# First attention layer of a four-layer attention and gMLP kernel: prologue order, weight burst, and two-tile residual loads

## The chip, the cores and the metric

The kernel runs on one core of a Trainium2 chip. The metric is the device time of one execution in microseconds (us). For each run except four early ones of the kernel before, the mean clock granted to TensorE is recorded as well, to three digits.

The engines are named as the profile names them: PE (TensorE matmuls), PEld (its weight loads), DVE (VectorE), ACT (ScalarE), POOL (GpSimd) and SP (SyncE). SPq, ACTq and POOLq stand for those engines' instruction queues when they issue a DMA.

## The reference

```python
x = A_x                                   # 2048 rows, 576 columns, bf16
x = x + A(layernorm(x))                   # attention, the layer that is changed
x = x + B(layernorm(x))                   # gMLP
x = x + A(layernorm(x))
x = x + B(layernorm(x))

def A(x):      # 32 heads of 18 columns; each row looks at 8 keys, 2 rows apart, behind it
    q, k, v = split(x @ wqkv)
    logits = sum(q[s] * k[s - 2*w] for the 18 columns) * 18**-0.5       # w = 0..7, masked at the start
    return (softmax(logits) @ v[s - 2*w]) @ wo

def B(x):      # F/2 = 2304
    z = gelu(x @ w_in)
    z1, z2 = z[:, :2304], layernorm(z[:, 2304:])
    return (z1 * (w_sp @ z2 + b_sp[:, None])) @ w_out
```

## The kernel before: what the change touches

The attention layer works in 19 row blocks t of 112 new rows, each in two steps (16 heads each), so steps s = 0 to 37. A step computes logits (`L_mm`, PE), exponentials (`EXP`, ACT) and the weighted values (`PV`, PE). A table hangs other PE work into the steps: query and key projections (`PG`), value projections (`VW`), output projections (`WO`).

Queries and keys need another layout than the projection leaves: each head at a multiple of 32 partitions. So `PG` evacuates into a staging tile, and DMAs of up to 18 partitions and 72 KB ("QK moves" below; half the size in the fifth block of columns) carry it into `QK`. Two of the staging tiles are lent by the later gMLP weight tile `win2a`; moves out of those are called QK<-win2a in the profile, moves from the others QK<-stg.

```python
# PG, when a staging tile is full: columns d*128.., half cb of the rows
for dst, src in moves:                                   # 18 partitions, 2 x 1024 columns of bf16
    dma_rr[0] += 1
    self.dma(dst, src, eng=queues[dma_rr[0] % len(queues)])     # POOL and SP in turn
...
def fill_window_rows(self, QK, half):                    # DVE copies of the window mask's rows into QK
...
# prologue of the first layer (cut): S_ statistics, E_/R_ 1/std, A_ normalize, T_pe transpose on PE
T_pe(0)                    # 5 transposes on PE, then an ACT copy into xnT
VW(0, 0, False)
VW(0, 1, False)
S_(2)
A_(1)
T_pe(1)
VW(1, 0, False)
S_(3)
...
rows[2](nc.scalar)         # ACT issues the store of the mask's rows, win_period
A_(2, 3)
T_pe(2)
T_pe(3)
VW(1, 1, False)
...
self.load_pat(nc.sync)     # reads win_period back
...
order = [(d, 0) for d in range(4)] + [(d, 1) for d in range(4)] + [(4, 0), (4, 1)]
for k_, (d, cc) in enumerate(order):                     # projections of the first 1024 rows
    for qk in ((1, 0) if d < 4 else (0,)):
        PG(d, qk, cc, False, (nc.gpsimd, nc.sync) if d in (0, 4) else q2)
...
T_(12, 13, 14, 15)         # DMA transposes, issued by SP
nvw0, nvw = 4, 8
...
self.fill_window_rows(QK, 1)                             # window rows of the second half

# the table: which PE work goes into which step
PG_END = 14
pre, pgs = pgs[:6], pgs[6:]
for k_, (d, qk, cc) in enumerate(pgs):                   # 12 projections of the last 1024 rows
    at((k_ * PG_END) // len(pgs), PG, d, qk, cc, True)
for t in range(nvw, NT):
    for hh in range(2):
        at(2 * t - 2 + hh, VW, t, hh, 2 * t - 2 + hh >= PG_END and hh == 0)
for i in range(NS):                                      # 16 tiles of 128 rows
    t = -(-(i + 1) * P // QT) - 1
    s = 2 * t + (6 if li == 0 and t < 8 else 5 if t < NT - 5 else 4 if t < NT - 3 else 3)
    at(s - 5, XO, i)       # SP loads the residual rows, one tile
    at(s, WO, i, 0)        # waits for oT<-o_t, a DMA transpose that SP issues
    at(s + 1, WO, i, 1)
    ...
    at(s + 4, LN_T, i)     # DMA transpose of the next layer's input, issued by SP
at(0, self.load_wo, nc.sync)
for k_, f in enumerate(self.load_win2a(nc.gpsimd)):      # six loads of 288 KB, issued by POOL
    at(5 + 2 * k_, f)
...
L_mm(0)
EXP(0)
for d, qk, cc in pre:      # six projections ahead of the logits of step 1
    PG(d, qk, cc, li > 0, q2)
for s in range(NST):
    if s + 1 < NST:
        L_mm(s + 1)
        EXP(s + 1)
    PV(s)
    for f, a in table.pop(s, []):
        f(*a)
```

The softmax here doesn't subtract the row's maximum and nothing guards it: scores larger than these inputs give would overflow.

## Time and profile before

| | before |
|---|---|
| median of the first three runs | 1196.32 us (1195.26 to 1196.66) |
| span of the profiled run | 1193.5 us, granted clock 0.999 |
| PE busy | 1180.0 us, 99% |
| PE idle outside the first 130 us | about 1 us (the second attention layer) and the tail |

From the page of the kernel before: the head and the first row of part 1 (busy time, share of the span, instructions), the clock row of part 2 (tenths of full speed in 40 slices), and part 4 (the chain that ended last, by engine).

```profile
span 1193.5 us, 20790 instructions
PE 1180.0 (99%) x8554; PEld 620.5 (52%) x8554; DVE 545.4 (46%) x1202; ACT 378.5 (32%) x597; POOL 274.3 (23%) x382
PEclk9999999999999999999999999999999999999999
PE 94%; DMA 1%; ACT 0%; issue 0%; DVE 0%; DVEq 0%; ACTq 0%
```

PE is the bound, so only time in which PE waits, or runs at a lower clock, can be won. The list of PE's waits (what waited, for whom: us in total, times, longest) is short:

```profile
PE pv L377 <- ACT xnT L567: 3.0, 3, 1.4
PE L_ps L435 <- ACT P_sb L444: 2.3, 6, 0.4
PE L_ps L435 <- DMA QK<-win2a: 1.9, 3, 1.0
...
PE pw L489 <- DMA oT<-o_t: 1.0, 1, 1.0
PE pw L489 <- DVE rec L461: 0.3, 1, 0.3
```

All but the exponentials' waits of the second attention layer lie in the first 110 us. The costliest place is at 47 us. The PE timeline there (start, duration, instruction, in brackets the idle time before it and what ended it):

```profile
47.86 0.20 PE L435 MATMUL L_ps<-QK 32*128 32x112 bf16 x1 [0.23 <-DMA QK<-win2a]
48.71 0.40 PE L435 MATMUL L_ps<-QK 32*128 32x112 bf16 x8 [0.65 <-DMA QK<-win2a]
50.08 0.22 PE L435 MATMUL L_ps<-QK 32*128 32x112 bf16 x1 [0.97 <-DMA QK<-win2a]
...
50.66 2.29 PE L400 MATMUL pp<-xnT,wqk_sb 128*128 128x512 bf16 x5
```

The logits of step 1 wait three times for the last QK moves. The projection that follows takes 2.29 us where the next takes 1.27: the records of the clock show one stretch of 3.41 us at half clock, 50.54 to 53.95 us. Such stretches are called half-clock windows below. One of them lowers the mean clock by 0.5 * 3.41 / 1193.5 = 0.0014.

What POOL and DVE did just before (their timelines; x5 means five instructions in a row, the duration covers all five):

```profile
41.77 4.82 POOL L77 DMA_DIRECT2D QK<-win2a  x5 [1.29 <-DMA QK<-stg]
40.88 4.62 DVE L197 COPY QK<-win_pat 128x4096 bf16<-128x4096 bf16 x4
```

POOL's five last move issues took 4.82 us, 0.96 us each in the mean, while DVE copied the window rows. Two more lines of this kernel are needed for the comparison below: the wait of an output projection at 104 us, and SP's issue of the last four QK moves.

```profile
104.10 0.79 PE L489 MATMUL pw<-wo_sb,oT 128*128 128x288 bf16 x5 [0.97 <-DMA oT<-o_t]
81.60 3.18 SPq L77 DMA_DIRECT2D QK<-stg  x4
```

### The profile page before, as it was taken

To read this page: it belongs to the slowest core of one execution; us is meant where nothing else is said; L and a number is where in the kernel's file an instruction comes from. 1 tells how busy PE (TensorE), PEld (TensorE's weight loads), DVE (VectorE), ACT (ScalarE), POOL (GpSimd) and SP (SyncE) were. 2 spreads that over 40 slices of the span, in tenths; PEclk is the share of its full clock that TensorE was granted. 3 is DMA by queue.
4 is the path that set the end of the run, shared out by engine and by line. 5 is a ranking of instruction groups with operands and counts; after the bars stand their busy time and mean duration, and the time that the engine had idled before them with its cause. 6 is when DMAs were issued, how large, how long until landed. Compare 5 with 4: busy or idle time off the path is not lost.

```text
span 1193.5 us, 20790 instructions
## 1 busy us (share of the span) xinstructions
PE 1180.0 (99%) x8554; PEld 620.5 (52%) x8554; DVE 545.4 (46%) x1202; ACT 378.5 (32%) x597; POOL 274.3 (23%) x382
## 2 busy tenths in 40 slices
PE   8999999999999999999999999999999999999998
PEld 5566644444444444457755775444444444444676
DVE  8577677333233233244455786763233233233321
ACT  5578677211111111201156786770110110111000
POOL 3568773100000000001153877530000000000000
PEclk9999999999999999999999999999999999999999
DMA  8799792000000000049645799900000000001332
GB/s 195 140 191 238 172 228 58 23 1 12 12 12 12 12 1 12 2 140 294 169 99 113 189 239 197 209 12 11 12 12 1 12 12 12 12 1 31 121 105 73
DMA packets 178791, 101.21 MB, mean 85 GB/s; under 512 B 135039, under 2 KB 160047, under 8 KB 178696
## 3 DMA queue, kind: packets, MB, share of 16 engines
q1 hardware_dynamic: 165400, 78.14, 29.4%
q0 software_dynamic: 6480, 15.99, 5.3%
q10 hardware_dynamic: 6816, 5.77, 1.6%
q8 instruction: 67, 1.10, 0.4%
q14 instruction: 28, 0.23, 0.1%
HBM read 42.39 MB, written 16.53 MB: 49 GB/s over the span
## 4 chain that ended last, share of the span: by engine, by line
PE 94%; DMA 1%; ACT 0%; issue 0%; DVE 0%; DVEq 0%; ACTq 0%
PE pg L878 42%; PE pz L860 12%; PE po L932 12%; PE pz L782 11%; PE pp L400 4%; PE pw L489 3%; PE O_ps L455 3%; PE pv L377 3%; PE L_ps L435 2%; PE pzs L782 1%; ACT P_sb L444 0%; DMA QK<-win2a 0%; DMA oT<-o_t 0%; PE pt L473 0%; DVE ln_st L218 0%
## 5 line engine op out<-in xcount | busy, mean ns | idle before, releaser
L878 PE MATMUL pg<-Wq,Z 128*128 128x512 bf16 x2304 | 502.8, 379 | 0.0
L878 PEld LDWEIGHTS <-Z 128*128 128x128 bf16 x2304 | 225.1, 98 | 272.2
L882 DVE TENSOR_TENSOR g_tmp<-pg,ln_xn 128x512 f32<-128x512 f32 x144 | 99.6, 692 | 428.0 <-PE pg L878 428.0
L872 ACT ACTIVATE z1T<-pz 128x1024 bf16<-128x1024 f32 x72 | 73.7, 1023 | 513.9 <-PE pz L860 513.7
L77 POOL DMA_DIRECT2D wout<-in_B_w_out_dram x4 | 4.2, 1060 | 604.6 <-PE pg L878 604.6
L932 PE MATMUL po<-wout,Z 128*128 128x288 bf16 x1152 | 141.4, 286 | 0.0
L444 ACT ACTIVATE P_sb<-L_ps 128x896 bf16<-128x896 f32 (+1 forms) x152 | 126.7, 888 | 41.8 <-PE L_ps L435 41.1
L860 PE MATMUL pz<-xnT,w 128*128 128x512 bf16 (+1 forms) x640 | 136.0, 380 | 0.0
L932 PEld LDWEIGHTS <-Z 128*128 128x128 bf16 x1152 | 112.7, 98 | 28.8
L782 PEld LDWEIGHTS <-xnT 128*128 128x128 bf16 (+1 forms) x800 | 66.3, 97 | 80.9 <-issue 23.7
L782 PE MATMUL pz<-win2a,xnT 128*128 128x512 bf16 x384 | 104.8, 380 | 0.0
L883 DVE TENSOR_TENSOR Z<-g_tmp,z1T 128x512 bf16<-128x512 f32 x144 | 99.7, 692 | 10.8 <-DVE g_tmp L882 1.4
L860 PEld LDWEIGHTS <-w 128*128 128x128 bf16 (+1 forms) x640 | 51.1, 97 | 80.0 <-issue 27.1
L400 PE MATMUL pp<-xnT,wqk_sb 128*128 128x512 bf16 x360 | 83.5, 382 | 0.0
L796 ACT ACTIVATE zp<-pz 128x1024 bf16<-128x1024 f32 x64 | 65.5, 1023 | 36.7 <-PE pz L782 34.1
L242 POOL TENSOR_SCALAR ln_xn<-x_new,ln_mv,ln_rstd 128x576 bf16<-128x576 f32 x32 | 73.3, 2291 | 2.7
L942 DVE TENSOR_TENSOR x_new<-po,xo 128x288 f32<-128x288 f32 (+1 forms) x64 | 28.8, 456 | 87.9 <-PE po L932 83.7
L782 PE MATMUL pz<-win2b,xnT 128*128 128x512 bf16 (+1 forms) x256 | 65.8, 380 | 0.0
L798 DVE CUSTOM_DVE_ANT_0 Z<-zp 128x1536 bf16<-128x1536 bf16 x32 | 56.3, 1760 | 16.2 <-ACT zp L796 16.1
L77 POOL DMA_DIRECT2D QK<-stg x81 | 50.0, 620 | 40.7 <-ACT P_sb L444 14.3
L377 PE MATMUL pv<-wv_sb,xnT 128*128 128x288 bf16 (+1 forms) x380 | 56.2, 285 | 3.0 <-ACT xnT L567 3.0
L400 PEld LDWEIGHTS <-wqk_sb 128*128 128x128 bf16 x360 | 33.3, 98 | 36.6 <-issue 0.8
(111 smaller groups left out, 889.0 us busy)
## 6 DMA issues: line engine op xcount, KB each, us to landing
xres<-x_new SPq DMA_DIRECT2D x48, 288.0 KB
xo<-xres SPq DMA_DIRECT2D x48, 288.0 KB
wout<-in_B_w_out_dram POOLq DMA_DIRECT2D x4, 1296.0 KB, 8.2
w<-in_B_w_in_dram SPq DMA_DIRECT2D x16, 256.0 KB
QK<-stg POOLq DMA_DIRECT2D x53, 72.0 KB, 4.1
QK<-stg SPq DMA_DIRECT2D x41, 72.0 KB
xo<-in_A_x_dram SPq DMA_DIRECT2D x16, 144.0 KB
win2a<-in_B_w_in_dram POOLq DMA_DIRECT2D x6, 288.0 KB, 5.0
```

What stands on the lines that cost most here:

```text
L242: e.tensor_scalar(out=xn[:nrows, 0:D], in0=x_t[:nrows, :], scalar1=mv[:nrows, 0:1], scalar2=rstd[:nrows, 0:1], op0=ALU.subtract, op1=ALU.mult)
L377: nc.tensor.matmul(pv[:nk, 0:288], lhsT=self.xnT[:, c, QT * t:QT * t + nk], rhs=wv_sb[:, c, hh * 288:(hh + 1) * 288], start=(c == 0), stop ...
L400: nc.tensor.matmul(pp[:, :], lhsT=w, rhs=self.xnT[:, c, PADL + cc * 512:PADL + (cc + 1) * 512], start=(c == 0), stop=(c == 4))
L444: nc.scalar.activation(out=P_bufs[(2 * s + jp) % 4][:nk, :, :, 0:nq], in_=Lv[:nk, :, :, 0:nq], func=ACT.Exp, scale=scale)
L782: nc.tensor.matmul(pzvs[ci][:, sub * 512:sub * 512 + w], lhsT=self.xnT[r0:r1, c, PADL + i * P:PADL + (i + 1) * P], rhs=win2(c)[r0:r1, c0 + ...
L796: nc.scalar.activation(out=zp[:, c0:c0 + cn], in_=pzvs[ci][:, 0:cn], func=ACT.Gelu_apprx_tanh, accum_out=sums[:, ci:ci + 1])
L860: nc.tensor.matmul(pz1s[q // 2][:, q % 2, :], lhsT=w1[r0:r1, c, sub * P:(sub + 1) * P], rhs=self.xnT[r0:r1, c, PADL + q * 512:PADL + (q + ...
L872: nc.scalar.activation(out=z1T[:, q2 * 512:(q2 + 2) * 512], in_=pz1s[q2 // 2][:, :, :].rearrange("p a b -> p (a b)"), func=ACT.Gelu_apprx_ ...
L878: nc.tensor.matmul(pg[:, :], lhsT=Z[:, jj, i, sub * P:(sub + 1) * P], rhs=Wq[q][:, i, :], start=(i == 0), stop=(i == NS - 1))
L882: nc.vector.tensor_tensor(out=tmp[:], in0=pg[:, :], in1=bsp[:, qs], op=ALU.add)
L883: nc.vector.tensor_tensor(out=uT(jj)[:, sub, qs], in0=tmp[:], in1=z1Ts[jj, sub][:, qs], op=ALU.mult)
L932: nc.tensor.matmul(acc[hh], lhsT=uT(j // 2)[:, j % 2, i * P:(i + 1) * P], rhs=wouts[j // NJH][:, j % NJH, hh * 288:(hh + 1) * 288], start= ...
```

## The change

Its intent: let no engine's queue stand still in the prologue, put the gMLP weight loads in one burst as soon as the lent staging tiles are free, and load residual rows two tiles at a time. With it come shifts in the table. The core of the diff, cut:

```diff
-            VW(0, 0, False)                      # prologue: tile 1 is transposed first
-            VW(0, 1, False)
             S_(2)
             A_(1)
             T_pe(1)
+            VW(0, 0, False)
+            VW(0, 1, False)
             VW(1, 0, False)
@@
-            rows[2](nc.scalar)
+            rows[2](nc.gpsimd)                   # POOL issues the win_period store
@@
-        if li == 0:
-            self.fill_window_rows(QK, 1)
@@
-            at((k_ * PG_END) // len(pgs), PG, d, qk, cc, True)
+            at(2 + k_ if li == 0 else (k_ * PG_END) // len(pgs), PG, d, qk, cc, True)
@@
-                at(2 * t - 2 + hh, VW, t, hh, 2 * t - 2 + hh >= PG_END and hh == 0)
+                if li == 0 and t == nvw:
+                    at(hh, VW, t, hh, True)
+                else:
+                    at(2 * t - 2 + hh, VW, t, hh, 2 * t - 2 + hh >= PG_END and hh == 0)
@@
-            s = 2 * t + (6 if li == 0 and t < 8 else 5 if t < NT - 5 else 4 if t < NT - 3 else 3)
+            s = 2 * t + (6 if li == 0 and t < 10 else 5 if t < NT - 5 else 4 if t < NT - 3 else 3)
@@
-            for k_, f in enumerate(self.load_win2a(nc.gpsimd)):
-                at(5 + 2 * k_, f)
+            for f in reversed(self.load_win2a(nc.gpsimd)):
+                at(0, f)                         # six loads in a burst
@@
-        L_mm(0)
-        EXP(0)
-        for d, qk, cc in pre:
-            PG(d, qk, cc, li > 0, q2)
+        for k_, (d, qk, cc) in enumerate(pre):
+            if k_ == (2 if li == 0 else 0):
+                L_mm(0)
+                EXP(0)
+            PG(d, qk, cc, li > 0 or k_ < 4, q2)  # four of them evacuated by DVE
+            if li == 0 and k_ == 3:
+                self.fill_window_rows(QK, 1)
```

Not shown: residual tiles of two row tiles (`XO` for even i loads rows i and i+1 in one DMA), buffers allocated early, the window-row scratch tile placed inside `oT`, and the additions of epsilon (`E_`) moved into `R_`.

More of the change, by code (lines that the diff above doesn't have):

```diff
@@ L113, in setup, with build_window_rows @@
         self.deferred = []
-    def build_window_rows(self, c):
+    def build_window_rows(self, c, R):
         nc = self.nc
-        R = c.tile([P, 2, MR, 16], bf16, name="win_rows")
         self.pat = self.consts.tile([P, 2, 272], bf16, name="win_pat")
@@ L342, in layer_A @@
         sb = sb_cm.__enter__()
+        x_news = [sb.tile([P, D], f32, name="x_new", tag="x_new", bufs=4) for k_ in range(4)]
+        xos = {k_: sb.tile([P, 2, D], x_prev_dt, name="xo", tag="xo", bufs=2) for k_ in range(2)}
         if self.right is None:
@@ L478, in XO @@
         def XO(i):
-            tails[i] = dict(xo=sb.tile([P, D], x_prev_dt, name="xo", tag="xo", bufs=3))
-            self.dma(tails[i]["xo"][:], x_prev[i * P:(i + 1) * P, :], eng=nc.sync)
+            if i % 2 == 0:
+                xo = xos.pop(i // 2, None) or sb.tile([P, 2, D], x_prev_dt, name="xo", tag="xo", bufs=2)
+                self.dma(xo[:], x_prev[i * P:(i + 2) * P, :].rearrange("(a p) d -> p a d", p=P), eng=nc.sync)
+                for k_ in range(2):
+                    tails[i + k_] = dict(xo=xo[:, k_, :])
         def WO(i, hh):
@@ L484, in WO @@
             if hh == 0:
-                st["x"] = sb.tile([P, D], f32, name="x_new", tag="x_new", bufs=4)
+                st["x"] = x_news[i] if i < 4 else sb.tile([P, D], f32, name="x_new", tag="x_new", bufs=4)
             r0 = (i % RING) * P
@@ L532, in layer_A @@
                 nc.tensor.matmul(warm[:, 0:P], lhsT=self.ident[:], rhs=self.ident[:], start=True, stop=True)
-            rows = self.build_window_rows(sb)
+            nR = 2 * MR * 16
+            rows = self.build_window_rows(
+                sb, oT[:].rearrange("p a b -> p (a b)")[:, 4 * D:4 * D + nR].rearrange("p (a r f) -> p a r f", a=2, r=MR))
             nc.scalar.copy(out=v_ext[:, :, :, DH:DH + 1], in_=self.ones[:, None, None, :].to_broadcast([P, NT, H, 1]))
@@ L544, in S_ @@
                     nc.vector.bn_aggr(out=mvs[:, i, :], in_=st[:])
-            def E_(i0, n):
-                nc.vector.tensor_scalar_add(out=rstds[:, i0:i0 + n], in0=mvs[:, i0:i0 + n, 1], scalar1=EPS)
             def R_(i0, n):
-                nc.gpsimd.tensor_tensor(out=rstds[:, i0:i0 + n], in0=rstds[:, i0:i0 + n],
-                                        in1=self.neg_half[:, 0:1].to_broadcast([P, n]), op=ALU.pow)
+                rs = rstds[:, i0:i0 + n]
+                nc.vector.tensor_scalar_add(out=rs, in0=mvs[:, i0:i0 + n, 1], scalar1=EPS)
+                nc.gpsimd.tensor_tensor(out=rs, in0=rs, in1=self.neg_half[:, 0:1].to_broadcast([P, n]), op=ALU.pow)
             xns = {}
@@ L572, in layer_A @@
             S_(0)
-            E_(0, 1)
             R_(0, 1)
             S_(1)
-            E_(1, 1)
             R_(1, 1)
@@ L584, in layer_A @@
             T_pe(1)
+            VW(0, 0, False)
+            VW(0, 1, False)
             VW(1, 0, False)
             S_(3)
-            E_(2, 2)
             R_(2, 2)
@@ L597, in layer_A @@
             S_(4, 5)
-            E_(4, 2)
             R_(4, 2)
@@ L605, in layer_A @@
             S_(7)
-            E_(6, 2)
             R_(6, 2)
@@ L612, in layer_A @@
             S_(9, 10, 11)
-            E_(8, 4)
             R_(8, 4)
@@ L619, in layer_A @@
             S_(13, 14, 15)
-            E_(12, 4)
             order = [(d, 0) for d in range(4)] + [(d, 1) for d in range(4)] + [(4, 0), (4, 1)]
```

## The prediction

> **What bounds the kernel now.** The page gives TensorE (PE) 99% busy, 1180.0 of 1193.5 us; the chain of waits is 94% PE. In the gMLP layers the waits view is empty. Winnable: about 13.5 us of PE idle and one clock dip, mostly in the first attention layer (windows, PE timeline):
>
> - Start: waits of 0.78, 0.81 and 1.44 us (3.0 in all) for ScalarE's (ACT) copy of xnT before the first projection matmul at 14.75 us. In the last, ACT issues the win_period store at 12.39 us, and copies transposed tiles 2 and 3 only from 12.77 us, though PE was done at about 11.4.
> - 47.3 to 50.2 us: PE waits 1.9 us for QK<-win2a DMAs. The last is issued by GpSimd (POOL) at 46.09 and lands at 50.04 us. Five such issues took 4.82 us (0.96 each, 0.59 in a quiet stretch), while VectorE's (DVE) QK<-win_pat copies ran (40.88 to 45.50 us). The Trainium skill, "SBUF — State Buffer", "SBUF: two separate sides", describes it: GpSimd cannot write DMA descriptors while DVE holds the shared ports. The trace agrees.
> - 50.54 to 53.95 us: granted clock 0.50 after that idleness; a five-matmul projection takes 2.14 us instead of 1.09 ("TensorE: Matmul & The Clock Gate", Part 1, has such an idle-window rule). Cost about 1.2 us.
> - Steps with little PE filler wait for exponentials: 0.74 us at 65, 0.42 at 82, 0.33 at 101. At 104 us an output projection waits 0.97 us for oT<-o_t, at 109 another 0.33 for rec.
>
> **What the change does.**
> 1. Prologue: tile 1 is transposed before the V matmuls, the win_period store leaves ACT for POOL. Projections start near 13.0 us. The second column group needs tiles 4 to 7, whose transposes, tied to DVE, are issued until 20.45 us; the lead may shrink. Gain 1.5 us (0.8 to 2.1).
> 2. The second half's window-row copies move behind the fourth early projection. POOL's last five issues lose about 1.9 us; PE arrives 1.5 us earlier, so a wait of about 1 us remains. Beyond step 1, gain 1.0 us, plus the clock dip at even chance: 0.6 us.
> 3. Output projections up to t=9 one step later: the 1.3 us at 104 to 109 mostly go. But V matmuls now sit in steps 0 and 1, steps 14 and 15 have no projection, 22 and 23 no output projection: six light steps of about 0.35 us (ACT-bound) in place of three (1.5 us). Net 0.5 us.
> 4. Burst of six win2a loads at step 0 (1.77 MB): they leave POOL's later stream and queue before QK<-stg moves not needed before about step 17. About 0.
> 5. Residual loads of two tiles: eight fewer SP issues of 0.5 us per attention layer; PE waits little there. About 0.2 us. The second attention layer (idle 0.9 us) hardly changes.
>
> Sum: about 3.8 us, nearly all on the critical path. Predicted **1192.5 us**, 8 in 10 between **1189.8** and **1195.0**. Chance of faster by over 2%: 0.01; within 2%: 0.98; slower by over 2%: 0.01.
>
> **Right if:** first projection near 13 us; wait on QK<-win2a under 1.2 us; POOL's last QK issues near 0.6 us; no wait on oT near 104 us; short ACT waits in steps 14, 15, 22, 23. **Wrong if:** the second column group stalls on xnT near 22 us; POOL's earlier queue, not the copies, sets the last QK landing; the burst delays other DMAs; the clock dips elsewhere.

## The result, and the profile after

The changed kernel took 1194.43 us (median of 4 runs, 1191.89 to 1195.45), the kernel before 1195.79 us (4 runs, 1194.83 to 1196.66). Ratios in this document are the mean time of one kernel's fast runs over the mean time of the other's fast runs of the same rounds, so they are not quite the ratio of the medians. Here it is 0.9986, with a 95% interval of 0.9968 to 1.0004: the same within the noise, by a hair faster.

The page of the changed kernel, the same rows:

```profile
span 1193.7 us, 20761 instructions
PE 1182.4 (99%) x8554; PEld 621.8 (52%) x8554; DVE 548.0 (46%) x1207; ACT 376.0 (31%) x592; POOL 275.3 (23%) x383
PEclk9899999999999999999999999999999999999999
PE 94%; DMA 2%; SPq 1%; POOL 1%; DVE 1%; issue 0%; ACT 0%; DVEq 0%; POOLq 0%
```

The second slice of the clock row, about 30 to 60 us, is now 8, and SPq appears in the chain. PE's waits:

```profile
PE L_ps L436 <- DMA QK<-win2a: 2.0, 3, 1.0
PE L_ps L436 <- DMA QK<-stg: 1.6, 2, 1.5
PE L_ps L436 <- ACT P_sb L445: 1.6, 4, 0.4
...
PE pt L569 <- DVE ln_xn L562: 1.1, 2, 0.7
PE pw L493 <- DMA oT<-o_t: 0.2, 1, 0.2
```

The 3.0 us for ACT's copy are gone, with 1.1 us for DVE in their place. The wait on QK<-win2a has not shrunk. The wait on QK<-stg is new. The PE timeline around the first of these:

```profile
46.65 0.20 PE L436 MATMUL L_ps<-QK 32*128 32x112 bf16 x1 [0.96 <-DMA QK<-win2a]
47.24 0.46 PE L436 MATMUL L_ps<-QK 32*128 32x112 bf16 x8 [0.39 <-DMA QK<-win2a]
48.38 0.27 PE L436 MATMUL L_ps<-QK 32*128 32x112 bf16 x1 [0.68 <-DMA QK<-win2a]
```

And around the new one:

```profile
90.84 0.22 PE L436 MATMUL L_ps<-QK 32*128 32x112 bf16 x1 [1.45 <-DMA QK<-stg]
91.22 0.22 PE L436 MATMUL L_ps<-QK 32*128 32x112 bf16 x1 [0.16 <-DMA QK<-stg]
...
91.79 1.19 PE L378 MATMUL pv<-wv_sb,xnT 128*128 128x288 bf16 x5
```

The last line took 1.19 us where the same five matmuls took 0.77 one step before: half clock again (92.00 to 95.42 us).

The most useful view is one that no single trace gives. I took the start of `PV` in each step from the PE timelines of both kernels; the difference is the lead of the changed kernel at that step. Since both run the same PE work in the end, the lead at the last step is what was won in this layer. At some steps the two have not yet done the same work: at step 24, for example, the changed kernel has one output projection of about 0.6 us still to do. There a lead moves without any wait.

| step | 0 | 3 | 8 | 13 | 15 | 17 | 18 | 19 | 23 | 24 | 28 | 36 |
|---|---|---|---|---|---|---|---|---|---|---|---|---|
| before, us | 50.23 | 57.60 | 67.80 | 80.44 | 84.73 | 89.06 | 91.24 | 93.37 | 101.94 | 105.15 | 114.22 | 132.01 |
| changed, us | 48.59 | 55.56 | 66.06 | 78.71 | 83.47 | 87.27 | 91.37 | 94.62 | 103.38 | 105.00 | 114.03 | 131.90 |
| lead, us | +1.64 | +2.04 | +1.74 | +1.73 | +1.26 | +1.79 | -0.13 | -1.25 | -1.44 | +0.15 | +0.19 | +0.11 |

So in this pair of traces the start won 2 us, the stall near 89 us and its half-clock window lost 3 us (from +1.79 to -1.25), and from step 23 to 28 1.6 us came back; the waits of the kernel before at 104 and 109 us, which the changed kernel does not have, are 1.3 us of that (0.97 and 0.33). The rest of the kernel, a thousand microseconds, adds nothing: the changed kernel's span ends 0.2 us behind.

Why was the last QK move late? SP's queue in the changed kernel, from 75 us (its DMA issues in order):

```profile
75.30 2.07 SPq L468 DMA_TRANSPOSE oT<-o_t  x1
77.46 3.29 SPq L77 DMA_DIRECT2D QK<-stg  x4
80.86 0.39 SPq L77 DMA_DIRECT2D xo<-in_A_x_dram  x1
81.36 1.24 SPq L248 DMA_TRANSPOSE xnT<-ln_xn  x1
82.65 0.57 SPq L77 DMA_DIRECT2D xres<-x_new  x1
83.32 1.97 SPq L468 DMA_TRANSPOSE oT<-o_t  x1
85.38 3.10 SPq L77 DMA_DIRECT2D QK<-stg  x4
```

SP is busy without a gap, and its last four moves are issued at 85.38 to 88.48 us, behind three transposes, the four moves of the projection before, a load and a store. In the kernel before the same four stood at 81.60 to 84.78 us; their projection sits one step earlier there (step 12, not 13). It is SP's moves that PE waits for: POOL's four of the same projection had landed by 87.79 us, before PE came to these logits at 89.01 us.

### The profile page after: what moved, and what is told of

Same layout as the page of the kernel before. It is cut to its first block, busy times and chain, and to the rows that moved or that the text cites. A ratio compares the mean times of both kernels' runs of the same rounds, so it can differ in the third digit from the quotient of the medians.

```text
span 1193.7 us, 20761 instructions
## 1 busy us (share of the span) xinstructions
PE 1182.4 (99%) x8554; PEld 621.8 (52%) x8554; DVE 548.0 (46%) x1207; ACT 376.0 (31%) x592; POOL 275.3 (23%) x383
## 4 chain that ended last, share of the span: by engine, by line
PE 94%; DMA 2%; SPq 1%; POOL 1%; DVE 1%; issue 0%; ACT 0%; DVEq 0%; POOLq 0%
PE pg L879 42%; PE pz L861 12%; PE po L933 12%; PE pz L783 11%; PE pp L401 4%; PE pw L493 3%; PE pv L378 3%; PE O_ps L456 3%; PE L_ps L436 2%; PE pzs L783 1%; SPq L77 1%; DMA QK<-win2a 1%; POOL QK L77 1%; DMA oT<-o_t 1%; DMA oT<-in_A_x_dram 1%
```

## The experiments

Theory A: the start gains about 2 us, which is given back at stalls on QK moves and on transposes, some of which bring half-clock windows; the rest is run-to-run scatter of the clock. Rivals: the moves are slow whatever the step (SP full, or the weight burst in the way); POOL's issues, not the moves, set the wait at 47 us; the time does not follow the clock.

Leads below are against the profiled run of the kernel before, as in the table above. Each experiment has one profiled and five timed runs, on the same chip as its runs of the kernel before. Different jobs ran on different chips.

### The changed kernel again, twice

> The changed kernel itself, for the spread of its runs. Theory A (clock): the 2.0 us won up to step 13 are given back at the stall near 89 us, and the time of a run is set by how many 3.4 us windows at half clock it has; so runs at clock 1.000 take about 1192 us, 0.999 about 1193, 0.997 about 1194, 0.996 about 1195.5, and the ratio to before is 0.998 to 0.999. Rival B (data movement alone): times do not follow the granted clock.

> The changed kernel once more, as company for the repaired one on the same chip. By my present theory its lead over the kernel before is about 2 us at PV of step 0, and 0 to 1.5 us from PV of step 28 on, since the output projections at steps 24 to 26 then wait for the transposes that SP issues; 1192 to 1195 us, ratio to before 0.998 to 1.000.

Edit: none. Measured: 1192.98 us against 1196.45 (ratio 0.9982, interval 0.9957 to 1.0007), and on another chip 1194.88 against 1195.94 (0.9994, 0.9976 to 1.0012). So the three comparisons give 0.9986, 0.9982 and 0.9994.

All runs of both kernels for which the record lists a clock (44 and 16), by clock:

| granted clock | before: runs, mean us | changed: runs, mean us |
|---|---|---|
| 1.000 | 11, 1193.57 | 4, 1191.90 |
| 0.999 | 10, 1195.16 | 4, 1193.85 |
| 0.998 | 7, 1195.37 | 1, 1193.94 |
| 0.997 | 8, 1197.11 | 3, 1195.59 |
| 0.996 | 5, 1198.36 | 4, 1197.16 |
| below | 3, 1199.19 | none |

The time follows the clock in both kernels. A straight-line fit over these 60 runs (the kernel and the clock as variables) gives 1.13 us for each 0.001 of clock, that is 1.6 us for one half-clock window, and 1.3 us for the change at equal clock. The mean clock of both kernels is the same, 0.998. So most of the scatter of 7 to 11 us between runs of one kernel goes with half-clock windows (correlation of time with clock -0.8 and -0.9), but the small gain does not: windows were not made rarer by the change. The fit mixes chips and says nothing on causes: a window follows PE waits, so a run with more waits has both.

The leads differ from run to run too. At step 28 they are +0.19, +1.31 and -1.38 us in the three profiled runs. In the second, PE is earlier (lead 3.18 us at step 25) and then an output projection waits 1.58 us at 107 us (the profile names a DVE instruction as its end, but the weight load beside it waited 1.9 us for oT<-o_t); in the third one waits 1.14 us for oT<-o_t at 110 us. That stall was not in the first trace: it belongs to the tile of block t=10, the first whose output projection the change did not move by one step.

### Prologue alone

```diff
 # kernel before
             T_pe(0)
-            VW(0, 0, False)
-            VW(0, 1, False)
             S_(2)
             A_(1)
             T_pe(1)
+            VW(0, 0, False)
+            VW(0, 1, False)
             VW(1, 0, False)
@@
-            rows[2](nc.scalar)
+            rows[2](nc.gpsimd)
```

> The kernel before with only two edits of the prologue: tile 1 is transposed before the V matmuls of block 0, and GpSimd, not ScalarE, issues the win_period store. First projection near 12.8 us instead of 14.75. If the QK moves' own speed sets their last landing (what the run with moves on ScalarE suggested), part of this is lost again at PV of step 0: lead there 0.5 to 1.5 us, the wait on QK<-win2a grows to 2 to 3 us. Time 1194 to 1196 us, 0 to 1.5 us faster than before.

Measured: the first projection starts at 12.87 us (14.75 before, 12.81 in the changed kernel), so these two edits are nearly the whole gain up to the first projection. The lead at step 0 is 0.98 us, at step 28 it is -1.27. Waits on oT<-o_t after 100 us total 2.1 us. 1195.98 us against 1195.16, ratio 0.9998 (0.9976 to 1.0019). In this trace two microseconds at 13 us are worth one at 50 us and none at the end.

### Window-row copies put back

```diff
+        if li == 0:
+            self.fill_window_rows(QK, 1)
@@
-            if li == 0 and k_ == 3:
-                self.fill_window_rows(QK, 1)
```

> The changed kernel with the window-row copies of the second half back ahead of the early projections. My prediction's term: GpSimd's last QK<-win2a issues slow to about 0.96 us each again while VectorE copies, the last one is issued 1 to 2 us later, and the wait on QK<-win2a grows from 2.0 to 3 to 4 us; 1195 to 1197 us. Rival: the moves in flight set the landing, and the copies cost the wait nothing (2.0 us, 1193 to 1195 us).

Measured: the wait on QK<-win2a was 1.3 us, not larger, but PE also waited 0.9 us for DVE to evacuate a projection, since DVE was copying. Together that is 2.2 us and the last moves landed at 49.11 us (48.38 in the changed kernel). The lead at step 0 is 0.67 us against 1.64, so the copies' place is worth 1.0 us there, the figure of the prediction (the changed kernel's own three traces differ by 0.7 us at this step); but by step 3 both leads are 2.0 us (1.99 and 2.04), because the half-clock windows fell differently. 1195.85 us against 1195.16, ratio 0.9992 (0.9969 to 1.0015). The expected growth of the wait did not show by itself; the test is not clean, as DVE evacuates here what ACT evacuated in the kernel before. POOL's nine last move issues ran without a pause here, from 38.24 to 45.87 us. In the changed kernel they took as long, from 37.57 to 45.31 us, with pauses in which POOL waited for earlier moves to land. So the prediction's reason, 1.9 us lost in POOL's queue, does not show here.

### Moves issued by ACT

```diff
-                    PG(d, qk, cc, False, (nc.gpsimd, nc.sync) if d in (0, 4) else q2)
+                    PG(d, qk, cc, False, (nc.scalar,) if d == 4 else (nc.gpsimd, nc.sync) if d == 0 else q2)
```

> The changed kernel with the moves QK<-win2a of the fifth column block, first half, issued by ScalarE, which is idle from 34 to 40 us, instead of GpSimd and SP. If GpSimd's queue (eight moves in flight, 0.6 us an issue) sets the last landing, the 2.0 us wait at 45.7 to 48.4 us and the half-clock windows after it go, and PV of step 0 starts near 46 us, not 48.6: 1190 to 1192 us if the stall near 89 us does not grow. If moves themselves are slow (6.5 us landings), the wait stays above 1 us: 1193.5 to 1195 us.

Measured: a failure. The wait on QK<-win2a grew to 2.9 us. ACT's queue of this kernel, and SP's:

```profile
34.35 8.61 ACTq L77 DMA_DIRECT2D QK<-win2a  x8
27.84 10.45 SPq L77 DMA_DIRECT2D QK<-stg  x9
```

Eight issues took ACT 8.61 us, and SP's nine took 10.45 us instead of 7.74. A third queue brought the moves no earlier. The Trainium skill, "DMA: Bandwidth & Descriptors", "Issuing engines are not separate DMA queues", says that spreading DMAs over engines saves only the issue time; here ACT's issues took 1.08 us each, SP's 1.16 in place of 0.86, and the last one of all queues ended at 44.04 us in place of 45.31. PE could still start the last logits only at 49.05 us (48.38 in the changed kernel). 1195.71 us, ratio 0.9993 (0.9967 to 1.0020). So POOL's queue alone does not set the landing; something common to all the moves does. Later, an output projection waits 2.82 us for oT<-o_t at 109 us, and the lead falls from 2.92 us at step 25 to -1.50 at step 28.

### Moves of half the size

```diff
-                cs = slice(PADL + cb * CBW, PADL + (cb + 1) * CBW)
+                NC = CBW // 2 if li == 0 and cb == 0 else CBW
+                cs = slice(PADL + cb * CBW, PADL + cb * CBW + NC)
@@ the three moves
-stg[s0:s0 + n, :, :]
+stg[s0:s0 + n, :, 0:NC]
```

> Wrong on purpose: the changed kernel with each QK move of the first half copying half of its columns; the issues, their order and the number in flight are unchanged. If the bytes of the moves set the last landing, the wait on QK<-win2a (2.0 us) falls below 0.7 us, no half-clock window follows it, and PV of step 0 starts near 46.5 us. If issue time or the limit of eight moves in flight sets it, the wait stays above 1.3 us. By theory A a kernel without the wait gains 2 us, plus up to 2.5 us where the windows went; 1190 to 1193 us.

The results are wrong, as meant (relative error 0.37). DMA issues of the changed kernel, POOL's 72 KB moves out of the lent tiles (size, median us from issue to landing), and then of this one, the same moves at half the size:

```profile
QK<-win2a POOLq DMA_DIRECT2D x4, 72.0 KB, 6.1
```

```profile
QK<-win2a POOLq DMA_DIRECT2D x4, 36.0 KB, 2.0
```

The wait on QK<-win2a is gone altogether, and the lead at step 0 is 4.22 us. The number and the order of the issues are the same, so the bytes in flight set the landing. They do so in part through POOL's queue: it no longer pauses for earlier moves to land, and its last move issue ends at 42.91 us in place of 45.31. That settles the wait at 47 us. Against the expectation, the half-clock window there did not go: there is still one at 51.04 to 54.45 us, after two other PE waits of 0.44 us (for ACT) and 0.68 us (for DVE).

But the time did not follow: 1195.94 us against 1194.01, ratio 1.0007 (0.9983 to 1.0032). The lead is 3.28 us at step 13, 2.21 at step 18, 4.02 at step 25, and 0.47 at step 28. Between the last two an output projection waits for oT<-o_t, followed by a half-clock window:

```profile
107.20 0.79 PE L494 MATMUL pw<-wo_sb,oT 128*128 128x288 bf16 x5 [2.05 <-DMA oT<-o_t]
```

Five traces keep the changed kernel's arrangement of output projections and reach step 25 with a lead of 2.8 us or more. All lose 1.7 to 5.2 us of it by step 28. This is a second bound, in the transposes that SP issues. It is not a fixed time: with the moves on ACT, with the dummies and with the old steps PE is 1.5 to 2.3 us behind the kernel before at step 28. One oT transpose held SP's queue for 1.22 us at 98 us and for 2.80 us at 102 us (dummies); why, was not tested.

### Dummy matmuls in the wait

```diff
+        if li == 0:
+            junk = self.PT_tile([P, 512], f32, "junk")
+            for _ in range(28):
+                nc.tensor.matmul(junk[:, 0:P], lhsT=self.ident[:], rhs=self.ident[:], start=True, stop=True)
         for s in range(NST):
             if s + 1 < NST:
                 L_mm(s + 1)
```

> The changed kernel with 28 dummy 128x128 matmuls just ahead of the logits of step 1, where TensorE waits 2.0 us for QK<-win2a: more work, no less waiting data. Theory A: the wait is filled, the half-clock windows at 47.6 to 54.5 us go, and the kernel gets 1 to 2.5 us faster than the changed one (1192 to 1193.5 us). Rival: if the wait itself is the whole cost and the clock costs nothing, 1194 to 1195 us, no faster.

Measured: 1195.81 us, ratio 0.9994 (0.9970 to 1.0018). The dummies took 1.73 us, but the wait behind them was still 2.1 us, since the last move landed at 49.74 us, 1.7 us later than in the run of the changed kernel in the same job (48.08). So the wait was not filled, and the test says nothing about the clock. There is no wait on QK<-stg near 89 us in this trace, but an output projection waits 2.53 us for oT<-o_t at 109 us, two half-clock windows follow, and the lead falls from 2.91 us at step 25 to -2.28 at step 28. Its three runs at clock 1.000 took 1193.3 us in the mean, those of the changed kernel in this job 1191.9. Why the landing came later is open; POOL's last issue came later (44.88 us against 44.09) and took longer (1.45 against 1.23 us).

### Projections at their old steps

```diff
-            at(2 + k_ if li == 0 else (k_ * PG_END) // len(pgs), PG, d, qk, cc, True)
+            at((k_ * PG_END) // len(pgs), PG, d, qk, cc, True)
@@
-                if li == 0 and t == nvw:
-                    at(hh, VW, t, hh, True)
-                else:
-                    at(2 * t - 2 + hh, VW, t, hh, 2 * t - 2 + hh >= PG_END and hh == 0)
+                at(2 * t - 2 + hh, VW, t, hh, 2 * t - 2 + hh >= PG_END and hh == 0)
```

> The changed kernel with the projections of the second half back at their steps of before (from step 0) and the V matmuls of row block 8 back at steps 14 and 15. Theory A: the wait on QK<-stg near 89 us (1.6 us) and its half-clock window go; in their place a projection at step 0 may wait for the transposes of the last four tiles, 0 to 1.5 us; 1191.5 to 1193.5 us. Rival B: the win2a burst or the full SP queue makes that wait, whatever the step; it stays, 1194 to 1195 us.

Measured: no wait on QK<-stg near 89 us; the lead does not change between steps 17 and 19 (-1.35 and -1.35). In its place the projection of step 0 waits 1.09 us for the transposes of the last tiles, two half-clock windows lie at 48.99 to 55.82 us, and later an output projection waits 1.98 us for oT<-o_t at 111 us. 1195.08 us, ratio 0.9992 (0.9972 to 1.0012). So without the late step there is no stall near 89 us, and the change had a reason to move the projections: the transposes are not there yet at step 0. The late step does not make the stall by itself: over the seven traces with this step and the burst, the listed wait on QK<-stg there is 1.6, 1.2, 1.1, 1.1, 0.6 us and twice none, as the moves are issued and land a little earlier or later.

### No burst

```diff
-            for f in reversed(self.load_win2a(nc.gpsimd)):
-                at(0, f)
+            for k_, f in enumerate(self.load_win2a(nc.gpsimd)):
+                at(5 + 2 * k_, f)
```

> The changed kernel with its six win2a loads spread over steps 5 to 15 as before, instead of one burst at step 0. My theory: the burst is neutral; waits near 47 and 89 us as in the changed kernel, same time within 1 us (1193 to 1195). Rival: the burst's 1.77 MB slow the moves and transposes in flight near 48 us, or block GpSimd; then the wait on QK<-win2a falls by over 0.5 us and the time by 1 us or more. Third: spread loads put back stalls at 100 to 109 us, 1 us slower.

Measured: 1199.99 us against 1195.16, ratio 1.0033 (1.0006 to 1.0061), the only variant that is slower clear of noise. The PE timeline and SP's queue of this kernel:

```profile
94.19 0.65 PE L436 MATMUL L_ps<-QK 32*128 32x112 bf16 x8 [4.61 <-DMA QK<-stg]
```

```profile
68.53 2.38 SPq L468 DMA_TRANSPOSE oT<-o_t  x1
71.02 3.30 SPq L77 DMA_DIRECT2D QK<-stg  x4
74.36 0.44 SPq L77 DMA_DIRECT2D xo<-in_A_x_dram  x1
74.92 2.21 SPq L468 DMA_TRANSPOSE oT<-o_t  x1
...
87.20 1.32 SPq L468 DMA_TRANSPOSE oT<-o_t  x1
88.61 3.10 SPq L77 DMA_DIRECT2D QK<-stg  x4
```

The last four moves are issued at 88.61 us instead of 85.38, and the stall near 89 us grows from 1.6 to 5.3 us (4.61 and a second of 0.66). SP's four oT transposes between 62 and 79 us took 2.15, 2.38, 2.21 and 1.97 us of its queue here; the same four in the changed kernel took 1.23, 2.07, 1.23 and 2.07. So the burst matters a good deal. The moves themselves were slower too: POOL's four of the last projection landed 5.8 to 6.7 us after their issue here and 3.7 to 4.4 us in the changed kernel. That the spread loads slow transposes and moves is the likely reason; the traces show them together but not the one making the other.

### Projections one step earlier, and output projections one step later

```diff
-            at(2 + k_ if li == 0 else (k_ * PG_END) // len(pgs), PG, d, qk, cc, True)
+            at(1 + k_ if li == 0 else (k_ * PG_END) // len(pgs), PG, d, qk, cc, True)
@@
-                    at(hh, VW, t, hh, True)
+                    at(0, VW, t, hh, True)
@@ in the second kernel only
-            s = 2 * t + (6 if li == 0 and t < 10 else 5 if t < NT - 5 else 4 if t < NT - 3 else 3)
+            s = 2 * t + (6 if li == 0 and t < 12 else 5 if t < NT - 5 else 4 if t < NT - 3 else 3)
```

> The changed kernel with only the projections of the second half one step earlier. If their lateness alone makes the stall near 89 us, the wait on QK<-stg there is under 0.3 us; the stall near 107 us on the output projection of t=10 (1.6 us in the second run of the changed kernel) stays or grows, as TensorE comes earlier. 1192 to 1194 us, between the changed kernel and the one with both repairs.

> The changed kernel with two repairs: projections of the second half one step earlier (steps 1 to 12, not 2 to 13), and output projections one step later up to t=11, not only t=9. If the stall near 89 us comes from the one step by which the last QK moves are late, and the one near 107 us (seen when TensorE is early) from the output projection of t=10 that was not moved, both go: waits on QK<-stg and oT under 0.3 us after 60 us, and 1190 to 1192.5 us. If SP's queue is simply full, they return elsewhere and the time is that of the changed kernel.

Measured, the first edit alone: no wait on QK<-stg after 60 us, but waits on the output projections of 2.7 us for oT<-o_t and 1.0 us besides; the lead falls from 3.94 us at step 18 to 1.21 at step 28. 1195.66 us against 1194.01, ratio 1.0003 (0.9982 to 1.0025).

Both edits: 1193.38 us against 1195.16, ratio 0.9976 (0.9954 to 0.9998). This is the kernel with the lowest mean. Its interval leaves out 1 only just, and it is one of thirteen comparisons. All PE waits between 60 and 130 us in its trace:

```profile
PE L_ps L436 <- ACT P_sb L445: 1.0, 3, 0.4
PE pw L493 <- DMA oT<-o_t: 0.5, 1, 0.5
```

The lead is 1.92 us at step 18, 3.43 at step 28 and 2.83 at step 36; span 1190.9 us. One more wait follows, 0.61 us for DVE at 131.5 us. So in this trace the two stalls were what took the gain. It was not run on one chip together with the changed kernel, so that it beats that one too is likely (1193.3 us mean of 6 runs against 1194.5 of 16) but not shown.

### Late transposes for the next layer

```diff
 # on top of both edits above
-                at(s + 4, LN_T, i)
+                at(s + (8 if li == 0 and i < 8 else 4), LN_T, i)
```

> The kernel with both repairs (projections one step earlier, output projections up to t=11 one step later) and a third: the xnT transposes of the first eight tiles, which nothing needs before the gMLP layer, are issued four steps later, so that they do not stand ahead of the oT transposes in SP's queue. If SP's order is what caps the lead, the lead over the kernel before at PV of step 28 is 3 us or more, no wait on oT over 0.5 us, and 1189.5 to 1192 us, ratio to before 0.995 to 0.998. If SP is simply full, the lead at step 28 is no more than the 3.4 us of the run without this third repair and a stall comes later, near 115 to 125 us.

Measured: 1193.18 us against 1195.94, ratio 0.9984 (0.9970 to 0.9999). The lead at step 28 is 3.65 us, then output projections wait 0.17 us at 115, 0.20 at 127 and 1.27 us at 133 us, and the lead at step 36 is 2.25. The wait at 133 us comes after that step, so less is left: the span is 1193.0 us, 0.5 us below that of the kernel before. Two more such waits, 0.50 and 0.69 us, lie at 86 and 91 us. The stall moved later, as the last sentence of the expectation had it; pushing transposes back in SP's queue made no room. The clock was 0.999 or 1.000 in all six runs, yet the time was no lower than without this edit (on another chip). So a better clock alone does not make a faster kernel.

## Why the prediction was right or wrong

Predicted 1192.5 us in a range of 1189.8 to 1195.0; measured 1194.43. The range held; the forecast gain of 3.8 us did not: it was 1.4 us by the medians, 1.3 at equal clock over all runs, and none of the three comparisons is clear of noise. That the range held is in part luck: its upper end lay only 0.8 us below the kernel before, and one of the four runs, at 1195.45 us, lies outside it. Point by point:

1. **Prologue, right.** Predicted start of the projections near 13.0 us, measured 12.81; no stall near 22 us. Alone it leaves a lead of 0.98 us at step 0.
2. **Wait at 47 us, mis-sized.** Predicted: a wait of about 1 us remains, lead at step 0 of 2.5 us (1.5 + 1.0). Measured: 2.0 us remain, lead 1.64. The prediction took POOL's issues, slowed by DVE's copies, as what sets the last landing. Without the copies in the way POOL waited for earlier moves to land instead, and with moves of half the size the wait vanished while the number and order of the issues stayed: the bytes in flight set it. Of its own signs of being right, the wait under 1.2 us failed; of its signs of being wrong, POOL's earlier queue as the setter came about in part. The mechanism that the Trainium skill describes in "SBUF — State Buffer", "SBUF: two separate sides" fits the 0.96 us per issue in the trace before, but that was not the wait that ended last.
3. **Half-clock window, given an even chance.** In the first trace there were three in place of one, one of them near 92 us ("the clock dips elsewhere" was a sign of being wrong); over all runs the mean clock is equal (0.998). The term of 0.6 us was not earned.
4. **Light steps, right in kind, too large.** Six waits of 0.35 us were predicted; the trace shows one wait of 0.43 us in each of the two pairs (83 and 103 us), 0.86 in all, less than the 1.5 us of before. The stalls at 104 and 109 us did go, as predicted: 1.3 us of waits, and 1.6 us of lead from step 23 to 28.
5. **Burst and late moves, wrong, and this is the step that cost most of the gain in the first trace.** The prediction put the burst at "about 0", with the moves "not needed before about step 17", and gave the later step of their projections no cost. The last moves are needed right then, by the logits of step 18, and with the one-step delay of their projection behind a full SP queue came a wait of 1.6 us plus a half-clock window: 3.0 us of lead in the first trace. The burst, costed at zero, is worth several microseconds in this arrangement, as the kernel without it shows (1.0033).
6. **What was missing altogether:** a second limit behind the first. A lead of 4 us at step 25 falls to 0.5 at step 28 when output projections still sit where SP's transposes just come in time. Moving them by one step for two more blocks kept 3.4 us there (2.8 at step 36).

Open: why the transposes hold SP's queue longer in some places, whether residual loads of two tiles did anything (they were not tried alone), why the move landings shift by up to 1 us between runs of one kernel, and what decides that a half-clock window follows.

## What to carry to other kernels

When PE is 99% busy, take the start time of the same step from both traces and subtract: the lead over time shows where a gain is made and where it is given back, which no total does. A queue that issues in order and is already full, as SP's was here, is a second critical path: moving any work that feeds it by one step has to be costed at the time at which its last DMA is needed, not at its mean load. And a gain of a microsecond at the start counts only after the next waits have been shown to move along with it.

## What the Trainium skill lacked or had wrong

- "DMA: Bandwidth & Descriptors", "Anatomy of one DMA — SWDGE (gpsimd) path" gives 2.0 us + bytes / 436e3. For 72 KB that is 2.2 us. With many 18-partition SBUF moves in flight, landings took 4.1 us in the median and up to 7.5; at half the size POOL's moves out of the lent tiles fell from 6.1 to 2.0 us. The page has no figure for many such moves at once.
- The same page, "Issuing engines are not separate DMA queues": the page has issuing from more engines save the issue time. Here the issues on ACT and SP grew: eight moves took ACT 8.61 us, and SP's nine went from 7.74 to 10.45 us, so that the last issue ended only 1.27 us earlier. The page does not say that they grow.
- No page says how long a DMA transpose holds the issuing queue beside other traffic. Here one of 112 or 128 x 640 bf16 held SP's queue for 1.2 us at the least and up to 3.9 us (with the projections at their old steps, at 120 us). These times add up in the queue that was the second bound.
- "TensorE: Matmul & The Clock Gate", Part 1, has the half clock come after an idle window of about 3.4 us. Here windows of 3.41 us at half clock followed 3.41 us in which PE was busy 1.56 us (before, 47.13 to 50.54), 2.06 and 1.80 us (changed kernel). Busy time alone does not decide it: 1.96 us busy at 9.58 to 12.99 us (before) brought none, 2.68 us busy at 62.54 to 65.95 us (prologue alone) did. These records show the length of the window as the page has it, and one window costs about 1.6 us of run time by the fit above.
